# 45 small loads of the gate's first weights, at three places of a decode kernel that streams 296 MB

## The chip, the cores and the metric

The kernel runs on one core of a Trainium2 chip. The metric is the device time of one execution in microseconds (us). Before the change it is 691.84 us, the median of 3 runs (691.77 to 691.97).

## The reference

One token (B = 1, D = 512) goes through attention over a cache (32 query heads, 8 K/V heads, 32768 cached positions, head width 128) and through a SwiGLU feed-forward layer (F = 1792). A gate, one number, mixes the two results. All data are float32.

```python
g = sigmoid((x * gate_w).sum(-1, keepdims=True))
q = (x @ wq)                                  # 32 heads of 128
scores = einsum("bhqd,bhkd->bhqk", q, k) * (Dh ** -0.5)
a = (softmax(scores) @ v) @ wo                # 4 query heads share one K/V head
b = (silu(x @ w1) * (x @ w3)) @ w2
out = g * a + (1 - g) * b
```

The K and V caches are 134 MB each and are read once. With wq, wo (8 MB each) and w1, w3, w2 (3.6 MB each) this makes some 296 MB.

## The kernel before

**Tiles and stages.** On-chip memory holds three large buffers, `ra`, `rb` and `rc`, each 128 partitions x 64 KB. Half a head of the K cache (8 MB) fills `ra` or `rb`; half a head of the V cache fills `rc`. At the start `rc` holds wq, and `rb` holds w1 and w3; at the end `rc` holds wo and `ra` holds w2, in five pieces (7, 4, 2 and 1 rows of 2 KB per partition, the last row in two halves of 1 KB).

**Loops.** For each of the 8 heads VectorE (DVE) transposes the K half in place (L355), TensorE (PE) multiplies it with the query (`scores`, L284), ScalarE (ACT) copies the scores and takes the exponentials (L393, L399), and one head later TensorE multiplies them with V (`values`, L298). GpSimd (POOL) lays out the next head's query in `winbuf` (L271). After the last head the attention result is multiplied with wo (L434), the hidden row of the feed-forward layer with w2 (L441, L451), DVE and ACT copy the row out (L471), and ACT stores it (L475).

**Order.** Everything is ordered by semaphores that are written out by hand. SP (SyncE) issues all large loads, in one fixed sequence: it waits until the buffer is free and issues the load. It stands still while it waits, so a later load is never issued ahead of an earlier one. Its DMA queue is q1 in the profile.

- L34: wq into `rc`, w1 and w3 into `rb`. L131 and L132: the first K half into `ra`, in two loads.
- L133 waits until the feed-forward products have read `rb`; L134 loads the second K half into it.
- L137 to L147, once per head: wait until `ra` is free (L137), K into `ra` (L138), V into `rc` (L143), K into `rb` (L145), V into `rc` (L147).
- L150 and L152: the last head's V halves into `ra` and `rb`, each behind a wait for TensorE.
- L156, L162, L165: wo into `rc`, w2 into `ra`.
- At the very end SP waits for ACT's last signal (L480), clears the semaphores and takes the output's completion.

ACT issues four small DMAs on its own queue, q10: x (one row of 2 KB, L168), the gate's weights (8 rows of 256 B, L169), a zero row to the output (L175) and the result (L475). After L175 its next work is the table load and the gate's sigmoid (L222), then 16 copies of the query into `winraw` (L231), for which POOL waits (L271), and then the feed-forward sigmoid (L254). DVE waits for the gate's sigmoid at L224, and only behind that transposes the query (L227).

**Completion.** A load raises its semaphore by 16 when all of it has landed, and its consumer waits for the 16. Each of the 16 DMA engines that takes part writes its share in a small packet of its own behind its data.

Of the kernel before, what the change touches and what calls it, by code (L numbers as in the profile page):

```python
# [24 lines left out]
@with_exitstack  # L25
def kernel(ctx, tc, x, k_cache, v_cache, wq, wo, w1, w3, w2, gate_w, out):
    nc = tc.nc
    rb, rc = (nc.alloc_sbuf_tensor(n, [P, 16384], F32).ap() for n in ("rb", "rc"))
    l_q, l_w1, l_w3 = (nc.alloc_semaphore(n) for n in ("l_q", "l_w1", "l_w3"))
    loads = [(rc, wq, l_q)]  # L30
    n = w1.shape[0] * w1.shape[1] // P
    loads += [(rb[:, i * n:(i + 1) * n], w, sem) for i, (w, sem) in enumerate(((w1, l_w1), (w3, l_w3)))]
    for to, w, sem in loads:
        i = nc.sync.dma_start(to, w.rearrange("(p c) n -> p (c n)", p=P)).then_inc(sem, 16)  # L34

        tc.no_tile_sem_insts.add(i.ins.name)
    tc.close()
    tc.compile()
    _program(nc, rb, rc, l_q, l_w1, l_w3, x, k_cache, v_cache, wq, wo, w1, w3, w2, gate_w, out)


def _program(nc, rb, rc, l_q, l_w1, l_w3, x, k_cache, v_cache, wq, wo, w1, w3, w2, gate_w, out):
    pe, dve, act, pool, sp = nc.tensor, nc.vector, nc.scalar, nc.gpsimd, nc.sync
# [13 lines left out]
    def sb(name, *shape):  # L57
        return nc.alloc_sbuf_tensor(name, [P, *shape], F32).ap()

    def token(name):  # L60
        return nc.alloc_semaphore(name)
# [41 lines left out]
    pq = [bank(3), bank(4)]  # L103


    l_x = token("l_x")
    l_a, l_a2, l_b, l_c = token("l_a"), token("l_a2"), token("l_b"), token("l_c")
    l_v = [token(f"l_v{i}") for i in range(2)]
    l_wo = [token(f"l_wo{i}") for i in range(2)]
# [14 lines left out]
    def take(sem, n=1, engine=pe):  # L124
        engine.wait_ge(sem, n).then_inc(sem, -n)  # L125


    kd = k_cache.rearrange("a h (p m n) d -> (a h) m p (n d)", p=P, m=2, n=NK)
    vd = v_cache.rearrange("a h (r p n) d -> (a h) r p (n d)", r=2, p=P, n=NK)
    half = W // 2  # L130
# [1 line left out]
    sp.dma_start(ra[:, half:W], kd[0, 0][:, half:W]).then_inc(l_a2, 16)  # L132
    sp.wait_ge(c_e.sem, 2)  # L133
    sp.dma_start(rb, kd[0, 1]).then_inc(l_b, 16)  # L134
    for h in range(HKV - 1):

        sp.wait_ge(c_k.sem, 2 * h + 1).then_inc(l_a2, 16)  # L137
        sp.dma_start(ra, kd[h + 1, 0]).then_inc(l_a, 16)  # L138
        if h:
            sp.wait_ge(c_v.sem, 2 * h)  # L140
        else:
            sp.wait_ge(c_act.sem, 2)
        sp.dma_start(rc, vd[h, 0]).then_inc(l_c, 16)  # L143
        sp.wait_ge(c_k.sem, 2 * h + 2)
        sp.dma_start(rb, kd[h + 1, 1]).then_inc(l_b, 16)  # L145
        sp.wait_ge(c_v.sem, 2 * h + 1)
        sp.dma_start(rc, vd[h, 1]).then_inc(l_c, 16)  # L147

    sp.wait_ge(c_k.sem, 2 * HKV - 1)
    sp.dma_start(ra, vd[HKV - 1, 0]).then_inc(l_v[0], 16)  # L150
    sp.wait_ge(c_k.sem, 2 * HKV)
    sp.dma_start(rb, vd[HKV - 1, 1]).then_inc(l_v[1], 16)  # L152
    wod = wo.rearrange("(p k) e -> p (k e)", k=32)
# [19 lines left out]
    n_zero = local.by(dve.memset(zero, 0.0))  # L173
    act.wait_ge(local.sem, n_zero)
    act.dma_start(od, zero).then_inc(l_out, 16)  # L175

    n_xp = local.by(dve.memset(xp, 0.0))
    n_ones = local.by(dve.memset(ones, 1.0))
# [32 lines left out]
    for c in range(NC):  # L211
        for b in range(2):
            for j in range(4):
                o = (c * HKV + 4 * b + j) * REP * DH
# [262 lines left out]

    act.wait_ge(done.sem, done.n).then_inc(t_end, 1)
    sp.wait_ge(t_end, 1)
    sp.sem_clear(range(l_q.num, l_out.num))  # L480
    take(l_out, 32, sp)

# [27 lines left out]
```

## Time and profile before

| | us |
|---|---|
| median of 3 runs | 691.84 |
| profiled execution, its span from the first to the last instruction | 690.5 |
| busy: TensorE matmuls (PE) | 380.2 |
| busy: VectorE (DVE) | 307.0 |
| busy: TensorE weight loads (PEld) | 107.8 |
| busy: ScalarE (ACT) | 41.7 |
| busy: GpSimd (POOL) | 7.1 |

The profile shows one execution. Of the profiled execution the span alone is given; the median of the runs lies 1.3 us above it. Times inside the execution count from the start of the span. On the page, the line that begins with DMA gives for 40 equal slices of the span how busy the core's 16 DMA engines were on the mean, in tenths. A DMA queue's row gives packets, megabytes, and the time that its packets took as a share of 16 engines over the span or the window asked for; where packets that start in a short window end behind it, the share can pass 100%. The list by time gives start, length, engine, line, operation and tiles, and in brackets how long the engine was idle before and what it waited for. SPq and ACTq are the instructions with which SP and ACT issue a DMA.

### The profile page before, as it was taken

To read this page: it belongs to the slowest core of one execution; us is meant where nothing else is said; L and a number is where in the kernel's file an instruction comes from. 1 tells how busy PE (TensorE), PEld (TensorE's weight loads), DVE (VectorE), ACT (ScalarE), POOL (GpSimd) and SP (SyncE) were. 2 spreads that over 40 slices of the span, in tenths; PEclk is the share of its full clock that TensorE was granted. 3 is DMA by queue.
4 is the path that set the end of the run, shared out by engine and by line. 5 is a ranking of instruction groups with operands and counts; after the bars stand their busy time and mean duration, and the time that the engine had idled before them with its cause. 6 is when DMAs were issued, how large, how long until landed. Compare 5 with 4: busy or idle time off the path is not lost. (4 is left out here: it accounts for less than half of the span.)

```text
span 690.5 us, 6710 instructions
## 1 busy us (share of the span) xinstructions
PE 380.2 (55%) x2946; PEld 107.8 (16%) x2946; DVE 307.0 (44%) x194; ACT 41.7 (6%) x111; POOL 7.1 (1%) x41
## 2 busy tenths in 40 slices
PE   1737256466463744567563735457463734466567
PEld 1200011103010121103020211103010211103122
DVE  1019378291725537091725447091815446191000
ACT  0020011002000010002000010002000010002000
POOL 0000000000000000000000000000000000000000
PEclk9975587879685876768577967778676966768678
DMA  9999999999999999999999999999999999999997
GB/s 410 400 434 455 425 430 430 448 440 429 426 429 437 425 437 444 437 429 425 433 433 433 444 440 429 425 429 437 429 444 440 433 425 429 437 425 437 441 417 318
DMA packets 6222, 296.35 MB, mean 429 GB/s; under 512 B 707, under 2 KB 963, under 8 KB 1094
## 3 DMA queue, kind: packets, MB, share of 16 engines
q1 hardware_dynamic: 6192, 296.23, 99.3%
q8 instruction: 6, 0.10, 0.1%
q14 instruction: 2, 0.02, 0.0%
q10 hardware_dynamic: 22, 0.01, 0.0%
HBM read 296.23 MB, written 0.00 MB: 429 GB/s over the span
## 5 line engine op out<-in xcount | busy, mean ns | idle before, releaser
L355 DVE STREAM_TRANSPOSE rb<-rb 128x2048 f32<-128x2048 f32 x64 | 141.8, 2274 | 150.3 <-DVEq L125 150.3
L284 PE MATMUL psum<-rb,winbuf 128*32 128x512 f32 x512 | 96.7, 836 | 122.9 <-PEq L125 122.9
L355 DVE STREAM_TRANSPOSE ra<-ra 128x2048 f32<-128x2048 f32 x64 | 141.4, 2276 | 43.0 <-DVEq L125 43.0
L298 PE MATMUL psum<-rc,prob 128*32 128x512 f32 x896 | 112.8, 660 | 41.3 <-PEq L125 41.3
L284 PE MATMUL psum<-ra,winbuf 128*32 128x512 f32 x512 | 87.5, 782 | 83.8 <-PEq L125 83.8
L298 PEld LDWEIGHTS psum<-rc,prob 128*32 128x32 f32 x896 | 33.6, 121 | 117.0 <-issue 116.8
L379 DVE TENSOR_REDUCE mx<-psum 128x4 f32<-128x1024 f32 x8 | 9.8, 1225 | 82.7 <-DVEq L125 82.7
L284 PEld LDWEIGHTS psum<-rb,winbuf 128*32 128x32 f32 x512 | 13.5, 125 | 202.7 <-issue 202.7
L393 ACT COPY sbuf<-psum 128x512 f32<-128x512 f32 x16 | 9.9, 618 | 478.0 <-PE psum L284 478.0
L284 PEld LDWEIGHTS psum<-ra,winbuf 128*32 128x32 f32 x512 | 14.9, 122 | 149.3 <-issue 149.3
L399 ACT ACTIVATE prob<-psum,nm 128x256 f32<-128x256 f32 x32 | 18.9, 695 | 39.3 <-DVE nm L387 39.3
L308 PE MATMUL psum<-ident,sbuf 128*64 128x64 f32 x512 | 16.7, 223 | 0.8 <-PEq L125 0.8
L308 PEld LDWEIGHTS psum<-ident,sbuf 128*64 128x64 f32 x512 | 15.6, 138 | 7.6 <-issue 7.6
L360 DVE SCALAR_TENSOR_TENSOR otall<-psum,gate,recip 128x4 f32 (+1 forms) x8 | 1.7, 214 | 32.8 <-DVEq L125 32.8
L298 PE MATMUL psum<-rb,prob 128*32 128x512 f32 x64 | 8.5, 690 | 9.7 <-DMA rb<-in_A_v_cache_dram 9.7
L215 PE MATMUL psum<-rc,xp 128*32 128x512 f32 x64 | 9.8, 782 | 4.7 <-DMA rc<-in_A_wq_dram 4.7
L434 PE MATMUL psum<-rc,oq 128*32 128x512 f32 x64 | 10.7, 829 | 2.6 <-DMA rc<-in_A_wo_dram 2.2
L271 POOL COPY winbuf<-winraw 32x16 f32<-32x16 f32 x32 | 6.1, 191 | 535.4 <-PE psum L284 499.7
L242 PE MATMUL psum<-rb,xp 128*32 128x448 f32 x64 | 8.6, 690 | 5.4 <-DMA rb<-in_B_w_dram 5.4
L298 PE MATMUL psum<-ra,prob 128*32 128x512 f32 x64 | 9.6, 770 | 3.3 <-DMA ra<-in_A_v_cache_dram 3.3
L200 PE MATMUL psum<-ones,ob 1*128 1x1 f32 x8 | 2.0, 370 | 15.2 <-DMA prob<-in_gate_w_dram 15.2
L318 PE MATMUL psum<-fold,ob 128*128 128x4 f32 x64 | 8.4, 255 | 0.8 <-PEq L125 0.8
(62 smaller groups left out, 79.0 us busy)
## 6 DMA issues: line engine op xcount, KB each, us to landing
ra<-in_A_k_cache_dram SPq DMA_DIRECT2D x2, 4096.0 KB, 52.6
rc<-in_A_wo_dram SPq DMA_DIRECT2D x2, 4096.0 KB, 45.5
rb<-in_B_w_dram SPq DMA_DIRECT2D x2, 3584.0 KB, 34.7
ra<-in_B_w_dram SPq DMA_DIRECT2D x1, 1792.0 KB, 33.4
ra<-in_B_w_dram SPq DMA_DIRECT2D x1, 1024.0 KB, 35.5
ra<-in_B_w_dram SPq DMA_DIRECT2D x1, 512.0 KB, 36.3
ra<-in_B_w_dram SPq DMA_DIRECT2D x2, 128.0 KB, 36.0
rc<-in_A_v_cache_dram SPq DMA_DIRECT2D x14, 30.4
```

The source lines that it names most:

```text
L215: m = pe.matmul(pq[b][32 * j:32 * j + 32, :], xp[:, c, :], rc[:, o:o + REP * DH], start=(c == 0), stop=(c == NC - 1),)
L242: i = pe.matmul(ps[32 * j:32 * j + 32, 0:FJ], xp[:, c, :], rb[:, o:o + FJ], start=(c == 0), stop=(c == NC - 1))
L271: pool.tensor_copy(winbuf[32 * r:32 * r + 32, 16:144].rearrange("p (c k) -> p c k", k=32)[:, :, 4 * r:4 * r + REP], winraw[32 * r:32 * r + ...
L284: i = pe.matmul(s_ps[m][32 * g:32 * g + 32, :], winbuf[:, w:w + 32], region.rearrange("p (n c i) -> p c n i", c=4, i=32)[:, c, n:n + 16], ...
L298: i = pe.matmul(o_ps[32 * t:32 * t + 32, :], prob[:, w:w + 32], region[:, n * DH:(n + 4) * DH], start=(r == 0 and g == 0 and f == 0), stop ...
L308: i = pe.matmul(pf[64 * s:64 * s + 64, 64 * a:64 * a + 64], sbuf[:, a].rearrange("p i m -> p (i m)"), ident.rearrange("p (gf r s q) -> p s ...
L318: i = pe.matmul(mb[:, 0:REP], ob[:, b * P:(b + 1) * P], fold[:, 4 * b:4 * b + 4], start=(b == 0), stop=(b == 3))
L355: dve.transpose(part[:, c], part[:, c]).then_inc(t_tr, 1)
L379: dve.tensor_reduce(mx, pf.rearrange("p (a q) -> p q a", q=REP), axis=AX.X, op=ALU.max).then_inc(t_mx, 1)
L393: act.copy(sbuf[:, :, :, m], s_ps[m].rearrange("p (n i) -> p n i", i=32)).then_inc(t_ev, 1)
L399: act.activation(prob[:, 0:1024].rearrange("p (a n q) -> p n a q", a=16, q=REP)[:, :, :, q], pf.rearrange("p (n a q) -> p n a q", n=16, q= ...
L434: pe.matmul(acc[32 * t:32 * t + 32, :], oq[:, k:k + 32], rc[:, k * D:(k + 1) * D], start=(k < 4), stop=False, skip_group_check=True,)
```

## The change

A helper, `marks`, issues 15 loads: for n from 1 to 15 it loads the first 2n weights of the gate, as n rows of 8 B, onto partition n of a new scratch tile, `diag`. Source rows lie next to each other; destination rows are 12 B apart. It is called three times: on SP behind L134 (the second K half into `rb`), on SP behind L150 (the last head's first V half into `ra`), and on ACT behind L175 (the zero row). Each place has its own columns of `diag`, and nothing reads the tile. All 45 loads raise one new semaphore, `l_d`, by 16 each; SP waits at the end for all of them, 720, before it clears the semaphores.

```diff
-    l_x = token("l_x")
+    l_x, l_d = token("l_x"), token("l_d")
+    diag = sb("diag", 135)
...
+    gw = gate_w.rearrange("(o d) -> o d", o=1)
+    n_marks = [0]
+
+    def marks(engine, place, w):
+        for n in range(1, 16):
+            o = 15 * (w + 1) * place
+            to = diag[n:n + 1, o:o + (w + 1) * n].rearrange("o (n w) -> o n w", n=n)
+            engine.dma_start(to[:, :, 0:w], gw[:, 0:n * w].rearrange("o (n w) -> o n w", n=n)).then_inc(l_d, 16)
+            n_marks[0] += 16
...
     sp.wait_ge(c_e.sem, 2)
     sp.dma_start(rb, kd[0, 1]).then_inc(l_b, 16)
+    marks(sp, 0, 2)
...
     sp.dma_start(ra, vd[HKV - 1, 0]).then_inc(l_v[0], 16)
+    marks(sp, 1, 2)
...
     act.dma_start(od, zero).then_inc(l_out, 16)
+    marks(act, 2, 2)
...
     act.wait_ge(done.sem, done.n).then_inc(t_end, 1)
     sp.wait_ge(t_end, 1)
+    sp.wait_ge(l_d, n_marks[0])
     sp.sem_clear(range(l_q.num, l_out.num))
```

## The prediction

> **What bounds the kernel now.** I read the head of the profile's page first, then the chain that ended last in order of time, then the waits of its last 15 us.
>
> ```profile
> span 690.5 us, 6710 instructions
> ...
> DMA  9999999999999999999999999999999999999997
> ...
> DMA packets 6222, 296.35 MB, mean 429 GB/s; under 512 B 707, under 2 KB 963, under 8 KB 1094
> ...
> q1 hardware_dynamic: 6192, 296.23, 99.3%
> ...
> q10 hardware_dynamic: 22, 0.01, 0.0%
> ```
>
> The 16 DMA engines are busy in every slice but the last. SP's queue (q1) alone fills 99.3% of them with 6192 packets, so the kernel moves its 296 MB with no hole into which added DMA work could go for free. ACT's queue (q10) has 22 packets: x, the zero row and the output are one row and one semaphore write each, the gate's 8 rows bring 8 and 8, and 2 + 2 + 2 + 16 = 22. So a load of n rows, at least for n = 1 and n = 8, is n data packets and n semaphore packets of 4 B, one pair to an engine.
>
> ```profile
> 677.63 2.14 another core or an unknown queue
> 679.78 0.04 issue
> 679.82 5.34 PE psum L434 x32
> ...
> 686.87 1.87 PE psum L451 x60
> ...
> PE psum L434 <- DMA rc<-in_A_wo_dram: 2.2, 1, 2.2
> ...
> PEld psum L451 <- DMA ra<-in_B_w_dram: 0.7, 1, 0.7
> ```
>
> In the chain (start, length, what) and the waits (total, times, longest) TensorE stands still for 2.2 us until the second half of wo has landed, and once more for 0.7 us until the last rows of w2 have. Both loads are the end of q1's stream. Whatever makes the slowest of the 16 engines later by some amount makes the end later by nearly that amount. The sum is therefore a sum over one DMA engine.
>
> **The change part by part.** It adds 45 loads, 15 at each of three places, of 1 to 15 rows of 8 B. It removes nothing and moves nothing. Each place has 1 + 2 + ... + 15 = 120 rows; with one pair of packets to a row, that is 240 packets, 720 in all, 480 on q1 and 240 on q10. Their bytes (720 times 8 or 4 B, under 5 KB) are nothing beside 296 MB; what counts is a price per packet.
>
> *Price of a packet.* I asked the DMA view for short windows in which few packets of one kind start; the share is of 16 engines over the window.
>
> ```profile
> DMA packets 65, 3.15 MB, mean 450 GB/s; under 512 B 16, under 2 KB 16, under 8 KB 17
> ...
> q1 hardware_dynamic: 48, 3.15, 103.7%
> ...
> DMA packets 8, 0.26 MB, mean 1053 GB/s; under 512 B 4, under 2 KB 4, under 8 KB 4
> ...
> q10 hardware_dynamic: 4, 0.00, 1.8%
> ...
> q10 hardware_dynamic: 3, 0.00, 0.9%
> ...
> DMA packets 10, 0.01 MB, mean 8 GB/s; under 512 B 4, under 2 KB 10, under 8 KB 10
> ...
> q1 hardware_dynamic: 10, 0.01, 2.4%
> ```
>
> From 7 to 14 us: 48 packets of 64 KB take 103.7% of 16 x 7 us, 2.42 us each. From 9.55 to 9.80: the gate's 4 rows of 256 B take 1.8% of 4.0 us, 18 ns each. From 9.89 to 10.08: 3 semaphore packets take 0.9% of 3.04 us, 9 ns each. From 687.8 to 688.6: the last 10 packets of w2, 4 of them 4 B and 6 of them 1 KB, take 2.4% of 12.8 us, 0.31 us; less 4 x 9 ns, a 1 KB packet takes 45 ns. A row of 8 B is not in the trace. It lies between the 4 B packet and the 256 B row, 9 to 18 ns, if it behaves like its neighbours; I take 9, since 8 B is nearest to 4 B. A gain from it is excluded: no packet goes away.
>
> *On which engine.* If every load starts at the same engine, that one gets a pair from all 45 loads, the next from 42, and so on to 3 at the fifteenth. The heaviest then carries 45 x (9 + 9) = 0.81 us, or 45 x (18 + 9) = 1.22 us with the upper price. Spread evenly, it would be 720 / 16 = 45 packets, 0.41 us. The Trainium skill, "DMA: Bandwidth & Descriptors" (Why a DMA increments its semaphore by 16 and not by 1), says that a load uses the largest number of engines up to 16 that divides its slowest dimension, and the lowest-numbered ones. By it the sum is the heavier 0.81 us and not 0.41; the 22 packets of q10 agree with the count for 1 and 8 rows, and no view here names the engines. I take 0.81 because nothing in the rows speaks for a rotation either.
>
> *How much of it reaches the end.* Only the engine that finishes wo and w2 last sets the end. The engines do not finish together:
>
> ```profile
> DMA packets 57, 0.07 MB, mean 131 GB/s; under 512 B 8, under 2 KB 52, under 8 KB 57
> ...
> DMA packets 49, 0.06 MB, mean 149 GB/s; under 512 B 6, under 2 KB 48, under 8 KB 48
> ```
>
> These are 686.9 to 687.4 and 687.4 to 687.8, ahead of the 10 packets above: the closing semaphore writes are strewn over more than a microsecond. The heaviest engine may have up to about that much to spare, or none. So 0 to 0.81 us comes through; I take half, +0.4 us.
>
> *Issue time.* Issuing a DMA holds its engine's sequencer.
>
> ```profile
> 0.73 0.37 SPq L34 DMA_DIRECT2D rc<-in_A_wq_dram  x1
> ...
> 2.86 0.53 ACTq L168 DMA_DIRECT2D ob<-in_A_x_dram  x1
> 3.22 0.43 SPq L132 DMA_DIRECT2D ra<-in_A_k_cache_dram  x1
> 3.42 0.73 ACTq L169 DMA_DIRECT2D prob<-in_gate_w_dram  x1
> 4.19 0.42 ACTq L175 DMA_DIRECT2D out_dram<-sbuf  x1
> 4.64 1.28 ACT L222 ACT_TABLE_LOAD   x1 [4.64 <-DVE ones L178]
> 18.19 0.17 ACT L222 ACTIVATE gate<-psum 128x1 f32<-128x1 f32 x1 [12.26 <-PE psum L209]
> ...
> 32.72 1.31 DVE L227 STREAM_TRANSPOSE rc<-psum 128x512 f32<-128x512 f32 x2 [14.18 <-PE psum L215]
> ...
> 46.50 0.33 SPq L134 DMA_DIRECT2D rb<-in_A_k_cache_dram  x1
> 70.81 0.33 SPq L138 DMA_DIRECT2D ra<-in_A_k_cache_dram  x1
> ...
> 595.27 0.33 SPq L150 DMA_DIRECT2D ra<-in_A_v_cache_dram  x1
> 622.27 0.33 SPq L152 DMA_DIRECT2D rb<-in_A_v_cache_dram  x1
> ```
>
> Between 0.42 us (one row) and 0.73 us (eight rows), 15 issues take 6.3 to 11.0 us. On SP the first place stands between 46.83 and 70.81, where SP waits 24.0 us for a free buffer anyway, and the second between 595.60 and 622.27, 26.7 us: both hidden. On ACT they begin at 4.61 and push the table load of 1.28 us; ACT's next work is the gate's sigmoid at 18.19, so 18.19 - 4.61 - 1.28 = 12.3 us are free. Were an issue dearer than 0.82 us, the sigmoid would be late, and next in line is DVE, which needs it before its transposes at 32.72: 14 us more of cover. All three places cost nothing.
>
> *Waits.* SP's wait for the 720 stands at the end behind the wait for ACT's last signal; the last small load was issued some 85 us earlier. Nothing.
>
> **Sum.** Profiled span 690.5 us + 0.4 = 690.9. The median of the runs, 691.84, is 1.3 us above the span, and with it the forecast is 692.24 us, about 692.2, with 691.7 to 693.1 (no effect to 1.22 us) as its own range. A measurement of this kernel can tell about 0.2%, 1.4 us, from no change.
>
> **The rivals.**
>
> *Tiny rows are dear (slower).* An 8 B row costs 31 ns or more with its semaphore write, the point at which 45 pairs reach 1.4 us with nothing to spare. The dearest near row is the 1 KB packet: 45 x (45 + 9) = 2.43 us, 694.3. If the 4 B write behind a tiny row costs as much too, 90 x 45 = 4.05 us, 695.9. For it: 240 packets in a row on one place with almost no bytes behind them are unlike anything here. Against it: 256 B at 18 ns is about the 9 ns of a 4 B packet plus the 256 B at the 64 KB packets' rate. The time then grows on one engine, all of it behind full queues, so the other 15 cannot help. Chance 0.17.
>
> *Rows are not spread one to an engine.* If only the largest power of two that divides n is used, engine 0 gets 1, 1, 3, 1, 5, 3, 7, 1, 9, 5, 11, 3, 13, 7, 15 rows, 85 a place. With 15 semaphore writes, 300 packets in all at 9 ns are 2.7 us (694.5), at 18 for a row 255 x 18 + 45 x 9 = 5.0 us (696.8). In this sense the change would not do what its row counts say. Nothing for it but that only 1 and 8 rows are shown, both powers of two. Chance 0.06.
>
> *Each tiny load is a round trip.* One engine takes up the next load only when the last has landed.
>
> ```profile
> 689.37 0.21 ACTq L475 DMA_DIRECT2D out_dram<-prob  x1
> ...
> q10 hardware_dynamic: 2, 0.00, 3.8%
> ```
>
> The output's issue ends at 689.58, and its 2 packets start between 690.05 and 690.20, so 0.47 us or more from issue to packet; 45 x 0.47 = 21 us, 713. Against it: the semaphore packets between the loads of w2 fit into the 2.4% above without a hole. The Trainium skill, "DMA: Bandwidth & Descriptors" (Latency and other measured facts), gives about 800 ns as the least that a tiny transfer takes, whatever its size; one behind the other that would be an estimate of 36 us, and the trace's back-to-back 4 B writes speak for latency that overlaps. Chance 0.03.
>
> *ACT's queue fills up (slower).* ACT's packets take turns with q1's of 64 KB, one per 2.42 us and engine. Engine 0 gets 6 packets from x, gate and zero and 30 from the third place. If the queue held only 8, ACT would issue its last after (36 - 8) x 2.42 = 68 us, at about 73.
>
> ```profile
> 34.07 4.06 ACT L231 COPY winraw<-rc 32x32 f32<-32x32 f32 x16 [15.71 <-DVE rc L227]
> 38.19 0.94 POOL L271 COPY winbuf<-winraw 32x16 f32<-32x16 f32 x4 [34.31 <-ACT winraw L231]
> ...
> 53.31 1.94 PE L284 MATMUL psum<-ra,winbuf 128*32 128x512 f32 x8 [6.88 <-PEq L125]
> ...
> rb<-in_A_k_cache_dram SPq DMA_DIRECT2D x1, 33.3
> ```
>
> The table load, the copies and POOL's would follow, 73 + 1.3 + 4.1 + 0.9 = 79, and the scores start at 79 instead of 53.3. The next K load goes out 26 us late, at 96.5, while rb's load has landed at 46.5 + 33.3 = 79.8: a hole of some 17 us, 709. It decides below 16 places: (36 - 16) x 2.42 = 48 us puts the scores at 60, and the K load at 77, ahead of 79.8. Against it: SP issues five loads, 8 rows and a semaphore write on each engine, 45 packets, between 0.73 and 3.65 us without a stall, so its queue holds more than 36. Chance 0.02.
>
> *Faster.* Only through drift of the engines against each other; nothing in the change frees anything. Chance 0.03, at about 690.
>
> **How the numbers follow.** The forecast has 0.69: all but a little of its own range lies within 0.2%, so same is 0.68. Slower takes the four rivals, 0.17 + 0.06 + 0.03 + 0.02, and 0.01 of the forecast's upper edge: 0.29. Faster 0.03. For the range I start at 691.5, just below no effect, and go up to 694.8: it takes in the 1 KB price and the lower end of the power-of-two case, and leaves out the round trips, the full queue and the dearest ends.
>
> **What would show it.** Step by step in the profile after: 6942 packets, 1427 of them under 512 B, 6672 on q1 and 262 on q10 (fewer: rows are not spread one to an engine); a short window just after rb's load in which the tiny packets' share gives 9 to 18 ns each; the issues as 15 in a row on SP and ACT, with L138 still near 70.8, L152 near 622.3 and the sigmoid near 18.2; scores still starting near 53.3. The prediction is wrong if the wait for wo grows by over 1.4 us, if a slice of the DMA row ahead of the last falls below 9, or if one of those four instructions has moved by more.

## The result and the profile after

The changed kernel takes 697.44 us, the median of 4 runs (696.24 to 697.69), beside 691.90 us for the kernel before: 5.5 us more, ratio 1.0077 (95% interval 1.0065 to 1.0089). The forecast was 692.2 with a range up to 694.8. The change is slower, and clearly so.

The head of the page of the changed kernel, line for line as shown of before:

```profile
span 696.3 us, 6756 instructions
...
DMA  9999999999999999999999999999999999999996
...
DMA packets 6943, 296.36 MB, mean 426 GB/s; under 512 B 1427, under 2 KB 1683, under 8 KB 1814
...
q1 hardware_dynamic: 6672, 296.23, 98.7%
...
q10 hardware_dynamic: 262, 0.01, 0.0%
```

The packet counts are those forecast for one pair per row: 1427 under 512 B, 6672 on q1, 262 on q10 (one more in all, an instruction fetch). The rows are spread as assumed. But q1's share has fallen from 99.3% to 98.7%: the engines now have time in which no packet is on record. At this grain the page can't say where.

SP's and ACT's issues, in order of time:

```profile
4.68 10.65 ACTq L136 DMA_DIRECT2D diag<-in_gate_w_dram  x15
15.36 1.28 ACT L236 ACT_TABLE_LOAD   x1 [15.36 <-issue]
18.35 0.17 ACT L236 ACTIVATE gate<-psum 128x1 f32<-128x1 f32 x1 [1.71 <-PE psum L223]
...
47.89 0.33 SPq L145 DMA_DIRECT2D rb<-in_A_k_cache_dram  x1
48.26 10.83 SPq L136 DMA_DIRECT2D diag<-in_gate_w_dram  x15
71.93 0.37 SPq L150 DMA_DIRECT2D ra<-in_A_k_cache_dram  x1
...
598.25 0.33 SPq L162 DMA_DIRECT2D ra<-in_A_v_cache_dram  x1
598.62 10.68 SPq L136 DMA_DIRECT2D diag<-in_gate_w_dram  x15
626.25 0.35 SPq L165 DMA_DIRECT2D rb<-in_A_v_cache_dram  x1
```

Issuing is innocent. It takes 0.71 us a load, inside the forecast span. ACT is done 1.7 us before its sigmoid, and SP is done more than 10 us before its next load at both places. Yet the second K half is issued 1.4 us later than before (46.50), and L165, the old L152, 4.0 us later (622.27): buffers come free later because loads land later.

The stretch of the first place in the DMA view, from 77 to 84 us, first before and then after:

```profile
DMA packets 63, 3.08 MB, mean 440 GB/s; under 512 B 16, under 2 KB 16, under 8 KB 16
...
q1 hardware_dynamic: 63, 3.08, 101.7%
```

```profile
DMA packets 291, 2.30 MB, mean 328 GB/s; under 512 B 256, under 2 KB 256, under 8 KB 256
...
q1 hardware_dynamic: 291, 2.30, 79.1%
```

The 240 tiny packets are there, but packets that start in this window now cover 22.6% of 16 x 7 us less than before: the engines stand idle between them. Such a share counts a packet whole where it starts, so it is rough at the window's ends. Adding up, from the packets of the kept traces, only the part of each that lies between 76 and 84 us gives the idle time itself: 20 us summed over the 16 engines, and none before. At the second place (636 to 645 us) the same count finds no idle time; there the loss hides elsewhere. Two windows of the changed kernel, 644.50 to 644.68 and 644.68 to 644.69:

```profile
DMA packets 32, 0.07 MB, mean 365 GB/s; under 512 B 31, under 2 KB 31, under 8 KB 31
...
q1 hardware_dynamic: 32, 0.07, 93.6%
...
DMA packets 1, 0.07 MB, mean 6554 GB/s; under 512 B 0, under 2 KB 0, under 8 KB 0
...
q1 hardware_dynamic: 1, 0.07, 2641.9%
```

In the first, 0.18 us hold 31 tiny packets back to back. Less the 2.42 us of a 64 KB packet that another engine starts among them, 93.6% of 16 x 0.18 us leaves 9 ns for each, as priced. In the second a single 64 KB packet starts; 2641.9% of 16 x 0.01 us is 4.23 us, where such a packet took 2.42. The loss of the last engine to pass this place is 1.81 us in the *next* packet's duration and 0.17 us in the tiny ones, 2.0 us in all.

This engine carries all 15 loads of the place. Each of the others can be followed too, from the end of one packet to the start of the next: the 16 engines have 1, 3, 5 and so on up to 31 tiny packets, two for each load and one semaphore write of the V half in front. That is the count if row r of every load goes to the same engine. Three of them, the windows 640.03 to 640.05, 640.895 to 640.905 and 643.125 to 643.135, each with the 64 KB packet that follows 4, 7 and 10 loads (a 9 ns packet is counted in the first and the last):

```profile
q1 hardware_dynamic: 2, 0.07, 765.3%
...
q1 hardware_dynamic: 1, 0.07, 1765.0%
...
q1 hardware_dynamic: 2, 0.07, 2265.6%
```

That is 2.44, 2.82 and 3.62 us. So the price is not the same for every load: behind four there is next to none, behind 7 it is 0.4 us, behind 10 1.2 and behind 15 1.8.

The chain of waits now ends on a load:

```profile
654.09 38.30 DMA ra<-in_B_w_dram
692.39 0.04 issue
692.43 2.14 PE psum L465 x60
```

The waits for loads have moved with it:

```profile
PEld psum L465 <- DMA ra<-in_B_w_dram: 1.6, 2, 1.4
PEld psum L455 <- DMA ra<-in_B_w_dram: 1.1, 1, 1.1
...
PEld psum L448 <- DMA rc<-in_A_wo_dram: 0.6, 1, 0.6
```

These are waits of TensorE's weight loads: 2.7 us for w2, where the kernel before had 0.7, and 0.6 us for wo, where it had 3.4.

### The profile page after: what moved, and what is told of

Same layout as the page of the kernel before. It is cut to its first block, busy times and chain, and to the rows that moved or that the text cites. A ratio compares the mean times of both kernels' runs of the same rounds, so it can differ in the third digit from the quotient of the medians.

```text
span 696.3 us, 6756 instructions
## 1 busy us (share of the span) xinstructions
PE 378.4 (54%) x2946; PEld 110.1 (16%) x2946; DVE 306.9 (44%) x194; ACT 41.8 (6%) x111; POOL 7.1 (1%) x41
## 2 busy tenths in 40 slices
DMA packets 6943, 296.36 MB, mean 426 GB/s; under 512 B 1427, under 2 KB 1683, under 8 KB 1814
## 3 DMA queue, kind: packets, MB, share of 16 engines
q1 hardware_dynamic: 6672, 296.23, 98.7%
## 5 line engine op out<-in xcount | busy, mean ns | idle before, releaser
L298 PE MATMUL psum<-rb,winbuf 128*32 128x512 f32 x512 | 94.4, 817 | 124.3 <-PEq L126 124.3
L312 PE MATMUL psum<-rc,prob 128*32 128x512 f32 x896 | 116.3, 677 | 42.2 <-PEq L126 42.2
L298 PE MATMUL psum<-ra,winbuf 128*32 128x512 f32 x512 | 82.7, 742 | 88.0 <-PEq L126 88.0
L322 PE MATMUL psum<-ident,sbuf 128*64 128x64 f32 x512 | 18.3, 235 | 0.8 <-PEq L126 0.8
L322 PEld LDWEIGHTS psum<-ident,sbuf 128*64 128x64 f32 x512 | 17.2, 149 | 8.4 <-issue 8.4
L312 PE MATMUL psum<-rb,prob 128*32 128x512 f32 x64 | 9.9, 788 | 12.6 <-DMA rb<-in_A_v_cache_dram 12.6
```

Source lines behind the costliest of these rows:

```text
L298: i = pe.matmul(s_ps[m][32 * g:32 * g + 32, :], winbuf[:, w:w + 32], region.rearrange("p (n c i) -> p c n i", c=4, i=32)[:, c, n:n + 16], ...
L312: i = pe.matmul(o_ps[32 * t:32 * t + 32, :], prob[:, w:w + 32], region[:, n * DH:(n + 4) * DH], start=(r == 0 and g == 0 and f == 0), stop ...
L322: i = pe.matmul(pf[64 * s:64 * s + 64, 64 * a:64 * a + 64], sbuf[:, a].rearrange("p i m -> p (i m)"), ident.rearrange("p (gf r s q) -> p s ...
```

## The experiments

In each timing the kernel before ran on the same chip (691.86 to 691.95 us); differences are against that median.

**One place at a time.** Three kernels, each with one call of the helper:

```diff
-    marks(sp, 1, 2)
-    marks(act, 2, 2)
```

and likewise with only the second SP place or only ACT's place left.

> Only the 15 loads behind the second K half (SP, first place) stay. Theory A, a price per tiny load on the engine that carries it, the same at every place: a third of the 5.5 us, +1.5 to +2 us over before. Theory B, crowding: what costs is that all engines reach the tiny loads at the same time and meet at the same 120 B of the source or the same partition; here they do, so this place alone gives +4 to +5.5 us, and its window of the profile shows DMA engines idle as in the changed kernel (79% busy from 77 to 84 us).

> Only the 15 loads behind the last head's first V half (SP, second place) stay. Theory A: +1.5 to +2 us, as at the first place. Theory B: without the first place the engines are not strewn when they come here, so they meet, and this place alone now costs what the first cost, +4 to +5.5 us, with idle engines in its window instead of the longer 64 KB packets of the changed kernel.

> Only the 15 loads on ACT's queue stay; their packets alternate with q1's. Theory A: +1.4 us, since L145 came 1.4 us later in the changed kernel, unless the engine has that much to spare until the end: +0 to +1.5 us. Theory B: packets that alternate with 28 to 64 KB packets do not meet, so +0 to +0.5 us.

| place left | median us | over before | ratio, 95% interval |
|---|---|---|---|
| first, SP | 694.04 | +2.1 | 1.0031 (1.0020 to 1.0042) |
| second, SP | 693.30 | +1.35 | 1.0019 (1.0009 to 1.0028) |
| ACT's | 692.83 | +0.9 | 1.0014 (1.0005 to 1.0023) |

Every place costs. The second alone, from 636 to 644 us, shows no hole:

```profile
q1 hardware_dynamic: 307, 3.34, 107.7%
```

So crowding is not something that any first visit brings; the first place did not reach the 4 us of theory B, and a plain equal price (theory A) does not give 2.1 against 1.35 either. The three add up to 4.3 us, not 5.5. Both theories needed mending.

**One engine alone.** First place, 15 loads of one row each.

```diff
-            to = diag[n:n + 1, o:o + (w + 1) * n].rearrange("o (n w) -> o n w", n=n)
-            engine.dma_start(to[:, :, 0:w], gw[:, 0:n * w].rearrange("o (n w) -> o n w", n=n)).then_inc(l_d, 16)
+            to = diag[n:n + 1, 0:w]
+            engine.dma_start(to, gw[:, 0:w]).then_inc(l_d, 16)
```

> First place alone, and each of its 15 loads has one row: one engine carries all 15 pairs, the other 14 none. Theory A: the heaviest engine carries the same 15 loads as in the run with the first place alone, so the same time. Theory B: no other engine is there to meet, so only what the second place showed in the changed kernel (0.13 us a load, 15 loads 2.0 us) or less: +0 to +2 us, clearly below the first place alone.

692.67 us, +0.7 (1.0010; 1.0001 to 1.0019). From 77.92 to 77.93 us:

```profile
DMA packets 2, 0.07 MB, mean 6554 GB/s; under 512 B 1, under 2 KB 1, under 8 KB 1
...
q1 hardware_dynamic: 2, 0.07, 2638.8%
```

These are one 4 B packet and the 64 KB packet behind the 30 tiny ones; 26.388 x 0.16 us less 9 ns is 4.21 us, 1.79 more than usual. With the tiny packets' own 0.18 us the engine loses 2.0 us, the loss seen at the second place: **0.13 us a load on the mean**, with no other engine near that carries small loads.

**Thirty loads.** The same with `range(1, 31)`.

> First place alone; 30 loads of one row of 8 B instead of 15, all on one engine. If that engine loses 0.14 us a load and has 1.4 us to spare until the end (15 loads lost it 2.15 us and the kernel 0.7): 4.3 us lost, +2.9 us. If the engine has no such time to spare and a load costs 0.05 us: +1.4 us, twice the 0.7.

694.84 us, +3.0 (1.0049; 1.0035 to 1.0062). From 78.09 to 78.10 us:

```profile
q1 hardware_dynamic: 2, 0.07, 4176.9%
```

The 64 KB packet now takes 6.67 us, 4.25 more than usual; with 0.35 us for the tiny ones the engine loses 4.6 us, 0.15 a load. The second 15 loads cost the kernel 2.3 us, the first 15 only 0.7. So this engine had 1.3 to 1.6 us to spare (2.0 - 0.7 and 4.6 - 3.0), and beyond that its loss comes through nearly one for one (2.3 of 2.6 us).

**Per load or per row.** One load with 15 rows on every engine, against 15 loads with one row on every engine:

```diff
+        to = diag[0:16, 0:45].rearrange("p (n w) -> p n w", n=15)
+        engine.dma_start(to[:, :, 0:w], gw[:, 0:480].rearrange("o (p n w) -> (o p) n w", p=16, n=15)).then_inc(l_d, 16)
```

```diff
+            o = 3 * (n - 1)
+            engine.dma_start(diag[0:16, o:o + w], gw[:, 0:16 * w].rearrange("o (p w) -> (o p) w", p=16)).then_inc(l_d, 16)
```

> First place alone; one load in place of 15: 16 partitions, 15 pieces of 8 B each, so every engine carries 15 tiny rows but one semaphore write. Per load (the semaphore write or the change of load is what holds the engine): one load, 0.14 us, +0 to +0.2 us. Per tiny row (each short read holds the engine's read-ahead): 15 rows on every engine, 2 us on all 16, nobody has time to spare, +2 us.

> First place alone; 15 loads of 16 rows on 16 partitions, so every engine carries 15 loads of one row and 15 semaphore writes. Both per load and per row 15 x 0.14 = 2.1 us on every engine, and no engine has time to spare: +2.0 to +2.2 us, where one engine alone gave +0.7. With crowding on top, all engines at once on the same 128 B, +3 us or more, and idle engines in the window from 76 to 84 us.

One load: 692.15 us, +0.3 (1.0004; 0.9995 to 1.0013), not to be told from nothing. Fifteen: 695.23 us, +3.35 (1.0052; 1.0038 to 1.0066). Both put 240 rows of 8 B at the same place. The two also differ in what they read, 1920 B against 128 B, so the profile is needed beside the times. With one load, three 64 KB packets start behind the tiny rows between 77.95 and 78.15 us, among 40 tiny packets:

```profile
q1 hardware_dynamic: 43, 0.20, 250.0%
```

250.0% of 16 x 0.2 us, less 40 x 9 ns, is 2.55 us for each of the three, 0.13 more than usual; behind 15 loads of one row on one engine it was 1.79 more. **The price is for the load, not for the row.** Whether the load's semaphore write or its start holds the engine was not separated. The 15 loads cost more than 15 x 0.14 us; their window from 76 to 84 us, behind that of before:

```profile
q1 hardware_dynamic: 65, 3.21, 92.8%
```

```profile
DMA packets 528, 2.10 MB, mean 263 GB/s; under 512 B 496, under 2 KB 496, under 8 KB 496
...
q1 hardware_dynamic: 528, 2.10, 66.0%
```

With all engines in step on the same 128 B the holes are back (34 us of idle time summed over the engines, counted as above, and 3 us with the one load), which speaks for a crowd on top.

**Where the crowd meets.** The first place with every row from its own address, and the first place with the rows of a load on separate partitions:

```diff
+        far = k_cache.rearrange("a h s d -> (a h s) d")[0:15 * 1021].rearrange("(o r x) d -> o r x d", o=1, x=1021)
...
+            engine.dma_start(to[:, :, 0:w], far[:, 0:n, 37 * n, 0:w]).then_inc(l_d, 16)
```

```diff
+            engine.dma_start(diag[0:n, o:o + w], gw[:, 0:n * w].rearrange("o (n w) -> (o n) w", n=n)).then_inc(l_d, 16)
```

> First place alone, its loads and engines unchanged, but every row comes from another address, half a MB apart (rows of the K cache). Crowding at the source: no engine meets another, the packets stand close together as at the second place, +1.3 us or less instead of +2.1. Crowding elsewhere, or none: +2.1 us again, with the engines idle between the tiny packets.

> First place alone, its loads and engines unchanged, but the n rows of a load go to n partitions, one to each, instead of all to partition n. Crowding at the partition written: +1.3 us or less, with tiny packets close together. Crowding at the source, or none: +2.1 us again.

Separate addresses: 693.23 us, +1.35 (1.0021; 1.0011 to 1.0030). Separate partitions: 694.23 us, +2.35 (1.0031; 1.0019 to 1.0043), no better than the first place as it was. The intervals overlap, so the profile has to decide. From 76 to 84 us, the first place as it was, then with separate addresses, then with separate partitions:

```profile
q1 hardware_dynamic: 300, 2.89, 87.2%
```

```profile
q1 hardware_dynamic: 301, 2.95, 95.7%
```

```profile
q1 hardware_dynamic: 300, 2.89, 90.5%
```

The kernel before has 92.8% in this window, so the shares alone can't decide either. Counted inside the window, the engines' idle time is 21 us, none, and 11 us. The hole goes with the shared address, and the place then costs what the second one costs. Separate partitions leave a hole; that it is smaller says little, for the same 15 loads left 8 us in the run with both SP places below.

"Shared" means that the engines read close together: in each load row r is the same 8 B of the 120 B and, by the counts at the second place, goes to the same engine, so the engines read neighbouring pieces and not one another's. The separate rows also lie in another tensor, the K cache. How far apart is far enough was not tried.

Why one place with separate addresses costs 1.35 us, and one engine with the same 15 loads only 0.7, can be read from the engine that passes the place last, from 79.14 to 79.16 us:

```profile
q1 hardware_dynamic: 2, 0.07, 1135.9%
```

Less a 9 ns packet this is a 64 KB packet of 3.63 us, 1.2 more than usual, behind ten loads. With the loads' own 0.12 us that engine loses 1.3 us, and as the last it has nothing to spare, which fits the 1.35. With the second place alone, too, one with ten loads passes last.

**Separate addresses at all three places**, the same edit to the whole change, and **ACT's place alone** with it:

> The change as it was, all three places, but every row from another address half a MB apart. Only the crowding at the first place goes (worth 0.75 us there alone): +4.5 to +4.9 us, and the window from 76 to 84 us has no tiny packets with idle time ahead of them. If crowding also costs at the other two places, below +4 us.

> Only ACT's 15 loads, and every row from another address half a MB apart. If the 0.9 us of ACT's place come from all rows being read at the same 120 B, they go: +0 to +0.3 us, and L145 is issued near 46.5 to 47 us. If they come from packets of a second queue in between, whatever they read: +0.9 us again.

All three: 694.51 us, +2.65 (1.0040; 1.0026 to 1.0054), well below the 4.5 expected and clear of the change's 1.0077. Its window from 77 to 84 us has no hole left:

```profile
DMA packets 298, 2.75 MB, mean 393 GB/s; under 512 B 256, under 2 KB 256, under 8 KB 256
...
q1 hardware_dynamic: 298, 2.75, 103.0%
```

ACT's place alone: 692.06 us, +0.15 (1.0002; 0.9993 to 1.0011), where it had cost 0.9; no run of the one (691.82 to 692.21) reaches the other (692.37 to 693.13). So ACT's loads cost only through the shared address. Two SP places at 2.0 us each less 1.3 to 1.6 us to spare make 2.4 to 2.7, the 2.65 measured; the engine with ten loads, at 1.3 us a place and nothing to spare, makes as much, and the run doesn't tell the two apart. **Of the 5.5 us, 2.65 are the price of the loads and 2.9 go when the 360 rows are no longer read from the same 120 B.**

**Both SP places, shared address.** Without `marks(act, 2, 2)`:

> Both places on SP, none on ACT, source as in the change. If the losses of the first engine add and only its 1.4 us to spare are taken off once: 2.1 + 1.4 = 3.5 us at the first place, 2.0 at the second, less 1.4: +4.1 us, and the last 1.4 of the 5.5 belong to ACT's place. If ACT's loads only made the crowding at the first place worse, or the places simply add with nothing to spare: +3.4 us (2.1 + 1.35).

695.59 us, +3.7 (1.0051; 1.0037 to 1.0065), between the two figures expected; the run doesn't tell them apart. ACT's place thus adds 1.9 us to the two others, though alone it costs 0.9. Whether its own loss merely finds no more spare time, or it also makes the crowd at the first place worse, stays open: the hole there is 8 us in this profile and 20 us in the changed kernel's, but with the first place alone it is 21.

**Longer rows.** One engine, 15 loads of one row of 1 KB, then of 4 KB, into a free part of `rc`; SP waits for them before it loads V there.

```diff
+        rows = k_cache.rearrange("a h (r x) d -> (a h r) (x d)", x=2)
...
+            engine.dma_start(rc[n:n + 1, 8192:8192 + 256], rows[1021 * n:1021 * n + 1]).then_inc(l_d, 16)
...
+        if h == 0:
+            sp.wait_ge(l_d, 240)
```

> First place alone; 15 loads of one row, all on one engine as in the run with one row each, but rows of 1 KB from the K cache, written to a part of rc that is free then (SP waits for them before it loads V into rc). Theory C, starting a load costs the engine 0.14 us that run beside the load's own data (the longer of the two counts): 15 x 0.14 = 2.1 us on that engine as with 8 B, of which its packets now show 15 x (46 + 9) ns = 0.8 us and the 64 KB packet behind them 1.3 us more than 2.42; +0.7 us. Theory D, the 0.14 us come on top of the data: 0.8 + 2.0 us, the 64 KB packet 1.8 to 2.0 us longer, +1.2 to +1.4 us.

> As before with rows of 4 KB, whose own 159 ns are more than 0.14 us. Theory C: the 64 KB packet behind them has its usual 2.42 us; the engine loses the 15 x (159 + 9) ns = 2.5 us of the data alone, +1.1 us. Theory D: the 64 KB packet is 1.8 to 2.0 us longer, 4.5 us on the engine, +3.1 us.

1 KB: 692.39 us, +0.5 (1.0007; 0.9998 to 1.0017). From 78.66 to 78.67 us, the packet behind the loads:

```profile
q1 hardware_dynamic: 1, 0.07, 2232.5%
```

That is 3.57 us, 1.15 more than usual, theory C's 1.3 and not theory D's 1.8 to 2.0. At this size the 0.13 us of a load run beside its own data. With 4 KB, 694.35 us, +2.5 (1.0037; 1.0023 to 1.0051), between C's 1.1 and D's 3.1. From 81.04 to 81.045 us:

```profile
q1 hardware_dynamic: 1, 0.07, 3455.0%
```

Here the packet behind takes 34.55 x 0.08 = 2.76 us, only 0.34 more than usual, so what D adds is not there. But the 15 loads themselves, followed from packet to packet, hold the engine for 3.4 us (77.66 to 81.04) and not for 2.5: the first six take 0.16 us each, as their data alone, and the nine behind them 0.27 on the mean. The engine thus loses 3.7 us, between C's 2.5 and D's 4.5; neither theory explains it. What slowed the later 4 KB loads was not tried.

## Why the prediction was wrong

- **What bounds the kernel: right.** The engine that ends last sets the end, and time lost on it beyond its spare comes through nearly one for one (15 against 30 loads). Of the signs of being wrong, L152 moved, by 4.0 us; the wait for wo shrank, and the one for w2 grew instead.
- **Packets and their spread: right.** The counts came out, and at the second place the engines carry 1, 3, 5 and so on up to 31 tiny packets. That one engine has the most of all three places is likely by this, but no view names the engines.
- **Price of a packet: this step failed.** It took the recorded duration of a packet, 9 ns for 4 B and 18 ns for 256 B, for all that the packet costs its engine. The 8 B packets do show 9 ns, but 15 or 30 loads with so little data cost their engine 0.13 to 0.15 us each on the mean, 7 to 8 times the 18 ns of the pair, and up to four of them next to nothing. The rest is in the next packet's duration or in idle time between packets, neither of which a window of tiny packets shows. The w2 rows quoted against a higher price could not have shown it: each semaphore write there follows eight packets of 1 KB, 8 x 45 ns = 0.36 us, long enough to cover it if it runs beside the data as in the 1 KB run.
- **The source address** had no term and no rival. It makes half of the loss.
- **What reaches the end:** half of up to a microsecond was taken as spare, on the heaviest engine; 1.3 to 1.6 us were there on the engine with all 15 loads of a place. This erred the other way and was small. With one place of separate addresses the engine that came last was not the heaviest but one with ten loads and nothing to spare.
- **Issue time and waits: right**, 10.65 to 10.83 us for 15 issues against 6.3 to 11.0, and covered at all three places.
- **The rivals.** "Tiny rows are dear" had the right sign and the right growth, on an engine behind full queues, but hung the price on the row, and its dearest figure, 90 ns a pair, was still too low. "Each tiny load is a round trip" had the right unit, the load, at 0.47 us; the loads overlap more than that. The rows not spread and ACT's full queue did not occur.
- The Trainium skill's rule on how a load is spread over engines, "DMA: Bandwidth & Descriptors" (Why a DMA increments its semaphore by 16 and not by 1), agrees with the packet counts after, 262 on q10 and 6672 on q1. The 800 ns that the Trainium skill gives for a tiny transfer ("DMA: Bandwidth & Descriptors", Latency and other measured facts) are not paid one behind the other: 30 loads cost 4.6 us.

## What to carry to other kernels

A packet's duration in a trace is not what it costs its DMA engine: price a kind of packet by what the next large packet behind it takes, and by the idle time between. Where DMA is the bound, count loads per engine and not bytes. Here up to four tiny loads in a row on an engine cost it next to nothing, and 15 to 30 of them 0.13 to 0.15 us each on the mean; loads of 1 to 15 rows put most of that on a few engines. Small loads that all read the same few bytes doubled the bill here; one load with many pieces cost next to nothing.

## What the runs showed of the hardware that was not expected

- Loads with one 8 B row cost their engine 0.13 to 0.15 us each on the mean, but four in a row cost next to nothing (2.44 us for the packet behind). 30 of them in front of a 64 KB packet stretch that packet's record from 2.42 to 6.67 us, while the tiny packets stand back to back at 9 ns.
- Reads of many engines within the same few bytes are slow: the same 45 loads cost 5.5 us from one 120 B and 2.65 us from separate addresses. On ACT's queue, where they run between large packets, the whole cost vanished with separate addresses (0.9 to 0.15 us).
- The second SP place did not show the holes, although it reads the same bytes. Nor is the hole at the first place steady: 21 us with that place alone, 8 us with both. How close in time the engines arrive may decide that; it was not tried by itself.
